# An attention and gated-MLP kernel on one core: a fixed order of all pieces, fewer bound products, and a transpose in two heights

## The chip, the core and the metric

The kernel runs on one core of one Trainium2 chip. A core has five engines that run side by side, each with its own queue of instructions, taken strictly in order: TensorE (PE) multiplies matrices into PSUM, with weight loads (PEld) beside the products; VectorE (DVE) reduces and combines; ScalarE (ACT) applies functions and copies out of PSUM; GpSimd (POOL) works on SBUF; SyncE (SP) here only issues transfers (DMAs). An instruction that waits holds up everything behind it in its queue.

The metric is the device time of one execution in microseconds. Before the change it was 249.93 (median of three runs, 248.54 to 249.93). About one per cent, 2.5 us, is what such a measurement can tell from no change.

## The reference

Two layers follow each other. The first is causal attention for 4 batches of 8 heads, 768 tokens, 64 values per head, in which each query sees only 6 of the 24 chunks of 32 keys: those with the largest upper bound of the score.

```python
ub = sum(max(q * k_min[chunk], q * k_max[chunk]))        # a bound per query and chunk
ub = where(own chunk or earlier, ub, -1e9)
top_chunks = argsort(ub)[-6:]
scores = where(in top_chunks and key <= query, scale * q @ k.T, -1e9)
attn = softmax(scores); x = attn @ v
```

The second layer is a gated MLP over tokens: `h = relu(x @ w_in)`, its halves are u and v; v is normalized over its 512 values, mixed over the tokens by `w_spatial`, a bias is added, and `out = (u * v_mixed) @ w_out`. The result is 4 x 768 x 512 floats.

A query in the first 128 tokens has at most 4 chunks at or before its own, so all of them are among its 6.

## The kernel before

Heads are taken in pairs, so that 2 x 64 values fill 128 rows: 16 pairs, four per batch. The work of a pair is cut into *pieces*, small functions `k_...` with one or a few instructions on one engine. A piece's name is its kind, its pair (or batch) and its part, as in `probs` (4, 512). In the order in which a pair needs them:

- `load`, `cast` (to 16 bits), `turn` and `kT`/`qT`: transposed keys and queries. Pairs 5 to 15 are transposed by a DMA from SP, the others by PE and a copy. `qp` is max(-q, 0).
- `ext` (DVE, L671): maximum and minimum of each chunk of keys. `bounds` (PE, L692 to L702): for each of six tiles of 128 queries, three kinds of products give the upper bounds of 24 chunks; for the first six pairs (`EARLY`) a further one adds a large negative number to chunks past the query (`big` times `far`). `ub` copies the result out of PSUM, and for later pairs adds that number there (`far32`). `top` (DVE) finds the eight largest for tiles 1 to 5, `leave` marks what is not among the first six.
- `pk` (PE) and `mx` (DVE, L792 to L808): the products of queries and keys and their largest value per chunk, kept in `cmax`. The first three pairs do it by another way (`kd`, `fd`, `fr`, `fi`, `fb`).
- `minus` and `kept` (POOL), `shift` (DVE): the softmax's shift is joined to the mask, as one table `bias`.
- `turn_bias` (PE, L826) transposes that table, `bT` (ACT) copies it out. `probs` (PE) are the scores plus mask, `ex` (ACT) their exponentials, `cut` (POOL) the causal mask in the diagonal blocks; it needs the first two parts of `ex`, 0 and 512. `weigh` (PE) multiplies by v, `av`, `sum`, `inv`, `norm` divide by the sums, and `xT` (by a DMA or by `turn_x` on PE and a copy) transposes the result.

When the four pairs of a batch are there, the second layer runs: `hv` and `hu` (the two halves of the first product), `vr` and `uT` (relu), `bn` and `rstd0` to `rstd2`, `vn` (normalizing), `mix` (over the tokens, by the transposed weights `wsT`, which `turn_ws` makes once), `plus` and `gT` (bias and gate), `og` (last product), `oe` (copy out of PSUM) and `od` (store).

Products on PE come in two heights. Those named in `TILED` (L102) use 64 rows, half the array, and stand in pairs on the two halves; all others use 128 rows.

*What sets the order.* `work_list()` (L251) lists 1395 pieces with their engines, an assumed duration, the pieces they follow, and the buffers they fill and read. `Work.order()` (L114) puts them in order. It walks a list: it keeps a clock per engine in assumed times, and whenever an engine is free it takes, of the pieces whose inputs are there and whose buffers can be had, the one with the lowest number in `RANK`. A piece that may run on more than one engine has its engine from a letter of `WHERE`. Each engine's queue is then this order, and each buffer's place is decided on the way (`place`, L139). The chip doesn't keep the assumed times: it keeps the order, and each instruction waits for its true inputs. PSUM holds three buffers `two` and two `mg`; kT and qT have four buffers, loads two.

Of the kernel before, what the change touches and what calls it, by code (L numbers as in the profile page):

```python
# [16 lines left out]
P = 128  # L17
# [66 lines left out]
"""  # L84
WHERE = """
AAAAGAGAGVGVGAAVAGAGAGVVAGAGAGAVVVVVAVAVAAAAAVVAVGGGGVGGAAVAAAAAAAAAAAVVAVAVVAAVAAVVGGGGGVVAAAAA
# [3 lines left out]
class Work:  # L90
# [8 lines left out]
    DELAY = {"PE": 0.25, "DVE": 0.17, "ACT": 0.18, "POOL": 0.14, "SP": 0.0}  # L99
    TILED = ("pk", "probs", "bounds", "turn_bias", "fd", "fb")  # L100
# [12 lines left out]

    def order(self):  # L114

        pieces, n = self.pieces, len(self.pieces)
        users, slot, freed_at, done_at = {}, {}, {}, {}
        slots = {tag: [None] * k for tag, k in self.bufs.items()}
        then, todo, ready_at, begun = [[] for _ in range(n)], [0] * n, [0.0] * n, [False] * n
        for i, (_, _, _, after, new, old, _) in enumerate(pieces):  # L120
            for b in new + old:
                users[b] = users.get(b, 0) + 1
            for a in after:
                then[self.index[a]].append(i)
                todo[i] += 1
        rank, where = [int(x) for x in RANK.split()], iter(WHERE.replace("\n", ""))
        engine = dict(P="PE", V="DVE", A="ACT", G="POOL", S="SP")
        assert len(rank) == n
        for i, (name, on, _, after, new, old, dma) in enumerate(pieces):
            if len(on) > 1:  # L130
                e = engine[next(where)]
                on = {e: on[e]}
# [934 lines left out]
```

## Time and profile before

| what | us |
|---|---|
| median of three runs | 249.93 |
| the profiled execution | 248.22 |
| its span, first to last instruction | 246.5 |
| PE busy | 224.9 |
| VectorE busy | 206.5 |
| ScalarE busy | 191.9 |
| GpSimd busy | 165.9 |

The page gives one execution. Its span is the time between the first and the last instruction, and the execution's own time is 1.7 us longer. Busy time is how long an engine had work in hand, whether or not the end of the kernel waited for that work. The clock that PE was granted is full in all of it. In a row of the timeline stand the start, the length, the engine, the line, the operation, its output and inputs, shapes, a count, and in brackets how long the engine was idle before it and who ended that. Products on PE overlap, so that the distance from one piece's start to the next piece's start, and not the length in the row, is what a piece takes.

### The profile page before, as it was taken

The page shows a single profiled execution, that of the slowest core. Times are in us where ns is not written, and L with a number is a line of the kernel's source. Part 1 is how long each engine was busy: PE and PEld are TensorE (multiplying, and loading weights), DVE is VectorE, ACT ScalarE, POOL GpSimd, SP SyncE. Part 2 cuts the span into 40 slices and gives each one's busy share as a digit, 9 for nine tenths or more (in the row PEclk, how much of TensorE's full clock was granted, in tenths as well). Part 3 has the DMA queues.
Part 4 walks back from the last instruction along what each step waited for, and adds up shares of the span by engine and source line. Part 5 has one row for each costly group of instructions (what it writes and reads, how often), then busy time and mean ns, then how long its engine had stood idle before and what let it go on. Part 6 is the DMA issues. An engine that isn't in the chain of part 4 may idle for free.

```text
span 246.5 us, 9019 instructions
## 1 busy us (share of the span) xinstructions
PE 224.9 (91%) x3780; PEld 144.6 (59%) x3780; DVE 206.5 (84%) x512; ACT 191.9 (78%) x298; POOL 165.9 (67%) x209
## 2 busy tenths in 40 slices
PE   0898778878999999999999999999999999999993
PEld 0656457666755675666665576666745566645551
DVE  4799999999999999799998997899998853349670
ACT  3598887979998999587859897897679969767312
POOL 8879749887785377999965929999926147402160
PEclk9999999999999999999999999999999999999999
DMA  7969996699999949484899997128900010350005
GB/s 189 325 186 201 257 242 127 122 164 241 168 186 235 216 82 187 89 170 112 190 161 271 175 200 125 34 75 140 268 22 19 0 36 0 105 188 0 0 28 227
DMA packets 93895, 35.51 MB, mean 144 GB/s; under 512 B 86208, under 2 KB 90144, under 8 KB 93856
## 3 DMA queue, kind: packets, MB, share of 16 engines
q1 hardware_dynamic: 91568, 31.81, 61.9%
q0 software_dynamic: 2016, 2.75, 6.5%
q8 instruction: 29, 0.48, 0.8%
q10 hardware_dynamic: 272, 0.39, 0.5%
q14 instruction: 10, 0.08, 0.1%
HBM read 24.77 MB, written 6.29 MB: 126 GB/s over the span
## 4 chain that ended last, share of the span: by engine, by line
PE 48%; DVE 28%; ACT 14%; DMA 4%; issue 3%; POOL 2%; DVEq 0%; ACTq 0%
DVE cmax L807 11%; PE mg L1001 11%; ACT pr L871 8%; PE mg L1024 6%; PE mg L885 5%; PE two L856 4%; PE mg L937 3%; PE two L863 3%; DVE stats L954 3%; DVE ext L671 3%; PE two L786 3%; DVE top L715 2%; PE mg L990 2%; DMA k<-in_k_dram 2%; DVE cmax L801 2%
## 5 line engine op out<-in xcount | busy, mean ns | idle before, releaser
L871 ACT ACTIVATE pr<-two 128x1024 f16<-128x1024 f32 (+1 forms) x96 | 85.3, 934 | 5.4 <-PE two L863 4.8
L807 DVE TENSOR_REDUCE cmax<-two 128x24 f32<-128x768 f32 (+4 forms) x104 | 85.3, 843 | 3.5 <-PE two L735 2.0
L856 PE MATMUL two<-qT,kT 64*128 64x128 f16 (+3 forms) x384 | 40.5, 258 | 5.4 <-ACT bT L835 1.9
L863 PE MATMUL two<-bT,member 64*128 64x128 f16 (+1 forms) x512 | 39.7, 233 | 0.0
L877 POOL TENSOR_SCALAR_AFFINE_SELECT pr<-pr 128x768 f16<-128x768 f16 x32 | 27.9, 886 | 9.1 <-ACT pr L871 9.0
L1019 POOL TENSOR_TENSOR vr<-tmp,uT 128x384 f16<-128x384 f32 x27 | 24.5, 922 | 11.9 <-DVE tmp L1012 11.8
L671 DVE TENSOR_REDUCE ext<-kT 128x24 f16<-128x768 f16 x32 | 29.5, 936 | 1.9 <-ACT kT L617 1.7
L1001 PE MATMUL mg<-wsT,vn 128*128 128x384 f16 x168 | 30.2, 327 | 0.0
L856 PEld LDWEIGHTS <-kT 64*128 64x128 f16 x384 | 19.9, 94 | 17.2 <-issue 15.1
L863 PEld LDWEIGHTS <-member 64*128 64x128 f16 x512 | 25.7, 94 | 5.1
L885 PE MATMUL mg<-v,pr 128*128 128x65 f16 x672 | 25.9, 194 | 0.7 <-POOL pr L877 0.5
L786 PE MATMUL two<-kT,qT 64*128 64x384 f16 (+4 forms) x182 | 24.6, 280 | 1.4 <-ACT pr L871 0.5
L885 PEld LDWEIGHTS <-pr 128*128 128x128 f16 x672 | 23.1, 98 | 3.6 <-issue 1.0
L1001 PEld LDWEIGHTS <-vn 128*128 128x128 f16 x192 | 17.7, 98 | 12.2 <-issue 0.6
L990 PE MATMUL mg<-xT,w_in_sb 128*128 128x384 f16 x112 | 22.4, 328 | 0.0
L907 POOL TENSOR_TENSOR x<-av,rc 128x768 f16<-128x768 f32 x11 | 16.2, 1469 | 8.8 <-DVE rc L900 4.9
L732 PE MATMUL two<-kT,qT 64*128 64x128 f16 x192 | 19.6, 221 | 2.3 <-ACT qT L617 1.0
L1024 PE MATMUL mg<-w_out_sb,vr 128*128 128x512 f16 x84 | 20.8, 380 | 0.0
L937 PE MATMUL mg<-w_in_sb,xT 128*128 128x512 f16 x84 | 20.3, 380 | 0.4 <-DVE o L619 0.4
L889 ACT COPY av<-mg 128x390 f32<-128x390 f32 x32 | 15.6, 500 | 6.2 <-PE mg L885 6.0
L954 DVE BATCH_NORM_STATS2 stats<-vr 128x6 f32<-128x512 f32 x24 | 16.6, 692 | 4.0 <-ACT vr L942 2.9
L735 PE MATMUL two<-half_ahead,ident 64*128 64x64 f16 x192 | 19.8, 193 | 0.0
(113 smaller groups left out, 496.8 us busy)
## 6 DMA issues: line engine op xcount, KB each, us to landing
q<-in_q_dram SPq DMA_DIRECT2D x16, 384.0 KB, 6.4
v<-in_v_dram SPq DMA_DIRECT2D x16, 384.0 KB, 5.7
out_dram<-o SPq DMA_DIRECT2D x24, 256.0 KB, 2.1
k<-in_k_dram SPq DMA_DIRECT2D x15, 384.0 KB, 5.7
vr<-in_moe_w_spatial_dram POOLq DMA_DIRECT2D x6, 192.0 KB, 5.6
w_in_sb<-in_moe_w_in_dram POOLq DMA_DIRECT2D x4, 256.0 KB, 8.8
w_out_sb<-in_moe_w_out_dram POOLq DMA_DIRECT2D x4, 128.0 KB, 4.5
k<-in_k_dram ACTq DMA_DIRECT2D x1, 384.0 KB, 4.7
```

Of the source, the lines that this page charges most:

```text
L671: nc.vector.tensor_reduce(held["ext", p][:, m], src, axis=AX.X, op=Alu.min if m else Alu.max, negate=(m == 1))
L786: mm(t[:, h, o:o + before], lhsT=qT[rows[h], c], rhs=kT[rows[h], a * CH:a * CH + before], start=True, stop=True)
L807: nc.vector.tensor_reduce(tops(p)[:, i // 2, :, i % 2, a:z], held["two", (p, u)][:, :, o:o + n].rearrange("p h (c e) -> p h c e", e=CH), a ...
L856: mm(t[:, h, z:z + n * P], lhsT=kT[rows[h], keys], rhs=qT[rows[h], i * P:(i + n) * P], start=True, stop=False)
L863: mm(d, lhsT=member[rows[h], r, keys], rhs=bT[rows[h], m * P:(m + w_) * P].rearrange("c (m s) -> c m s", s=P), start=False, stop=(n == 1 o ...
L871: nc.scalar.activation(out=held["pr", p][:, :, c0:c0 + n], in_=held["two", (p, "e", c0)][:, :, 0:n], func=Act.Exp, scale=scale)
L877: nc.gpsimd.affine_select(out=d, in_=d, compare_op=Alu.is_ge, fill=0.0, base=0, channel_multiplier=-1, pattern=[[0, NT], [1, P]])
L885: mm(a[:, i, :], lhsT=pr[:, at[t, i]:at[t, i] + P], rhs=vp[:, h * NT + t, :], start=(t == 0), stop=(t == i))
L937: mm(t, lhsT=held["xT", b][:, ko, i * P:(i + 1) * P], rhs=w_in_sb[:, ko, DH:2 * DH], start=(ko == 0), stop=(ko == NDO - 1))
L990: mm(t, lhsT=w_in_sb[:, ko, db * P:(db + 1) * P], rhs=held["xT", b][:, ko, s * HS:(s + 1) * HS], start=(ko == 0), stop=(ko == NDO - 1))
L1001: mm(t, lhsT=held["vn", b][:, si, db * P:(db + 1) * P], rhs=wsT[:, si, s * HS:(s + 1) * HS], start=(si == 0), stop=(si == NT - 1))
L1024: mm(t, lhsT=held["vr", ("g", b)][:, ko, i * P:(i + 1) * P], rhs=w_out_sb[:, ko, :], start=(ko == 0), stop=(ko == KO - 1))
```

## The change

Four things change.

1. `Work.order()` no longer walks a list with clocks. `RANK` now holds the place of each piece in one order of all pieces, and the function only reads it off, asserts that inputs come first, and gives each buffer the place whose last use lies furthest back. The numbers in `RANK` and the letters in `WHERE` are new, so nearly every piece moves a few places, and some pieces change engine.
2. `bounds` leaves out the three products of the first tile. Only the `big` times `far` product stays there, now for all pairs.
3. `turn_bias` can use all 128 rows: for those pairs whose `turn_bias` stands between two pieces of the other height in PE's queue, it multiplies by 64 columns of the whole identity and not by the half's own.
4. Assumed durations in `work_list()` are altered; with no clock left in `order()`, they have no effect.

```diff
+    EITHER = ("turn_bias",)
...
     def order(self):
...
-        free = {e: 0.0 for e in self.ENGINES}
-        ready = {e: [] for e in self.ENGINES}
-        events = [(0.0, i) for i in range(n) if todo[i] == 0]
...
+        for (name, on, _, _, _, _, _), at in zip(pieces, rank):
+            result[at] = name, engine[next(where)] if len(on) > 1 else next(iter(on)), at
+        done = set()
+        for at, (name, _, _) in enumerate(result):
+            _, _, _, after, new, old, _ = pieces[self.index[name]]
+            assert all(a in done for a in after) and all(b in slot for b in old), name
+            for b in new:
+                tenants = held[b[0]]
+                free = [(-1 if x is None else last[x], k) for k, x in enumerate(tenants) if x is None or users[x] == 0]
+                assert free, name
+                slot[b] = min(free)[1]
+                tenants[slot[b]] = b
...
     order, slot = work.order()
+    turned = [name for name, e, _ in order if e == "PE"]
+    whole = {name[1] for a, name, z in zip(turned, turned[1:], turned[2:])
+             if name[0] in Work.EITHER and not (a[0] in Work.TILED or z[0] in Work.TILED)}
...
-            each = [(big, far[:, i])] * (p < EARLY) + [(qT[:, c], x[:, 0]), (qp[:, c], x[:, 0]), (qp[:, c], x[:, 1])]
+            each = [(big, far[:, i])] * (p < EARLY or i == 0) + [(qT[:, c], x[:, 0]), (qp[:, c], x[:, 0]), (qp[:, c], x[:, 1])] * (i > 0)
...
-                r = slice(g * D, (g + 1) * D)
-                mm(t[:, g, m * D:(m + 1) * D], lhsT=bias[slot["bias", p]][r, 4 * m:4 * m + 4, :].rearrange("p g c -> p (g c)"), rhs=ident[r, r], start=True, stop=True)
+                r, c = slice(g * D, (g + 1) * D), slice(0, P)
+                if p in whole:
+                    r, c = c, r
+                mm(t[:, g, m * D:(m + 1) * D], lhsT=bias[slot["bias", p]][r, 4 * m:4 * m + 4, :].rearrange("p g c -> p (g c)"),
+                   rhs=ident[r, c] if p in whole else ident[r, r], start=True, stop=True)
```

What moves, in the built order of each engine:

- SP: the first loads were q0, v0, k2, q1, k1, q2 and become q0, q1, k1, k2, v0, q2. The transfer of `member` and the load of the MLP's bias come later.
- POOL: `rows` (which builds `member`) comes after `cast` of q1, k1, k2 and `kd` 0; `cast` of v2 after `kept` 2; `far32` after the cuts of pair 1; the last load of the spatial weights behind `norm` 2.
- ACT: the six parts of `ex` 15 came as 0, 1024, 2048, 1536, 2560, 512 and come as 0, 512, 2048, 1024, 2560, 1536.
- PE: most pieces move by one to six places; `turn_ws` 4 comes ahead of `pk` (6,0) and `weigh` (3,1); `turn_x` 15 comes before the last `og` of batch 2 and not after it.
- Engines: `kT` 0 goes from ACT to DVE and `ub` 3 and 4 from DVE to ACT; `norm` 6 and 7 from POOL to DVE, `norm` 13 from DVE to POOL; `qp` 8 and 13 from ACT to DVE, `qp` 14 back; `oe` (0,1), (0,3), (1,3), (1,4) from DVE to ACT; and 16 pieces of the second layer in batches 2 and 3.

More of the change, by code (lines that the diff above doesn't have):

```diff
@@ L1 @@
-import heapq
 import math
@@ L32 @@
 RANK = """
[51 rows of a table removed]
[51 rows of a table added]
 """
 WHERE = """
-AAAAGAGAGVGVGAAVAGAGAGVVAGAGAGAVVVVVAVAVAAAAAVVAVGGGGVGGAAVAAAAAAAAAAAVVAVAVVAAVAAVVGGGGGVVAAAAA
+VAAAGAGAGAGAGAAVAVAVVGVVAGAGAGVGAVVVAAAAAAAAAAAAVGGGGVGVAAAVAAAAVAAAVVVVAVAVAAAVVVVGGVGVGGAVAVAA
 """
@@ L116, in order @@
         pieces, n = self.pieces, len(self.pieces)
[L117 to L120, printed above, removed]
+        rank, where = [int(x) for x in RANK.split()], iter(WHERE.replace("\n", ""))
+        engine = dict(P="PE", V="DVE", A="ACT", G="POOL", S="SP")
+        assert sorted(rank) == list(range(n))
@@ L121, in order @@
+        users, slot, last, result = {}, {}, {}, [None] * n
+        held = {tag: [None] * k for tag, k in self.bufs.items()}
+        for _, _, _, _, new, old, _ in pieces:
             for b in new + old:
                 users[b] = users.get(b, 0) + 1
[L123 to L132, printed above, removed]
-            pieces[i] = (name, on, rank[i], after, new, old, dma)
-        free = {e: 0.0 for e in self.ENGINES}
-        ready = {e: [] for e in self.ENGINES}
-        events = [(0.0, i) for i in range(n) if todo[i] == 0]
-        t, bus, late, tiled, result = 0.0, 0.0, 0.0, False, []
-        def place(i):
-            got = []
-            if any(b not in slot for b in pieces[i][5]):
-                return None
-            for tag, key in pieces[i][4]:
-                for k, b in enumerate(slots[tag]):
-                    if b is None or freed_at.get(b, t + 1) <= t + 1e-9:
-                        got.append(((tag, key), k))
-                        break
-                else:
-                    return None
-            return got
@@ L153, in begin @@
-        def begin(e):
-            nonlocal bus, late, tiled
-            aside, found = [], False
-            while ready[e] and not found:
-                due, i = heapq.heappop(ready[e])
-                if begun[i]:
-                    continue
-                got = place(i)
-                if got is None:
-                    aside.append((due, i))
-                    continue
-                found = begun[i] = True
-                name, on, _, _, new, old, dma = pieces[i]
-                result.append((name, e, t))
-                took = on[e]
-                if e == "PE" and tiled != (name[0] in self.TILED):
-                    tiled, took = not tiled, took + 0.095
-                free[e] = t + took
-                if dma:
-                    if e == "POOL":
-                        late = max(late, t + took + 0.2)
-                        both = max(0.0, bus - late)
-                        bus += min(both, dma)
-                        late += 4 * dma if dma <= 0.25 * both else 0.75 * both + dma
-                        done = late + 0.8
-                    else:
-                        bus = max(bus, t + took + 0.4)
-                        both = max(0.0, late - bus)
-                        bus += 4 * dma if dma <= 0.25 * both else 0.75 * both + dma
-                        done = bus + 0.8
-                else:
-                    done = t + took + self.DELAY[e]
-                for b, k in got:
-                    slot[b] = k
-                    slots[b[0]][k] = b
-                for b in new + old:
-                    done_at[b] = max(done_at.get(b, 0.0), done)
-                    users[b] -= 1
-                    if users[b] == 0:
-                        freed_at[b] = done_at[b]
-                        heapq.heappush(events, (freed_at[b], -1))
-                for j in then[i]:
-                    todo[j] -= 1
-                    ready_at[j] = max(ready_at[j], done)
-                    if todo[j] == 0:
-                        heapq.heappush(events, (ready_at[j], j))
-            for x in aside:
-                heapq.heappush(ready[e], x)
-            return found
@@ L203, in order @@
-        heapq.heapify(events)
-        while len(result) < n:
-            while events and events[0][0] <= t + 1e-9:
-                i = heapq.heappop(events)[1]
-                if i >= 0:
-                    for e in pieces[i][1]:
-                        heapq.heappush(ready[e], (pieces[i][2], i))
-            while any([free[e] <= t + 1e-9 and begin(e) for e in self.ENGINES]):
-                pass
-            later = [f for f in free.values() if f > t + 1e-9] + [e[0] for e in events[:1]]
-            assert later or len(result) == n, "nothing can go on"
-            t = max(t, min(later, default=t))
+        for (name, on, _, _, _, _, _), at in zip(pieces, rank):
+            result[at] = name, engine[next(where)] if len(on) > 1 else next(iter(on)), at
@@ new lines, in order @@
+        done = set()
[8 more added lines that the diff above has]
+                tenants[slot[b]] = b
+            for b in new + old:
+                users[b] -= 1
+                last[b] = at
+            done.add(name)
@@ L318, in work_list @@
         far_pe = p < EARLY
-        add("bounds", {"PE": (6 * far_pe + 18) * 0.027},
+        add("bounds", {"PE": 0.54 if far_pe else 0.412},
             DUE["bounds"],
@@ L396, in work_list @@
                 add("inv", {"DVE": 0.14}, at, 0, after=[("sum", p, 0)], old=[("rc", (p, 0))])
-                add("norm", {"POOL": 1.6, "DVE": 1.45}, at, 0, after=[("inv", p, 0)], old=[("av", p), ("rc", (p, 0))], new=[("x", p)])
+                add("norm", {"POOL": 1.5, "DVE": 1.15}, at, 0, after=[("inv", p, 0)], old=[("av", p), ("rc", (p, 0))], new=[("x", p)])
                 continue
```

8 lines of the change are left out of this document (4 added, 4 removed), and 102 rows, old and new, of the table RANK.

## The prediction

> **What bounds the kernel now.** I read the page's header, its slices and its chain first, then the busy time by stage, then the waits inside the stages. PE is TensorE, DVE VectorE, ACT ScalarE, POOL GpSimd.
>
> ```profile
> span 246.5 us, 9019 instructions
> ...
> PE   0898778878999999999999999999999999999993
> ...
> DVE  4799999999999999799998997899998853349670
> ...
> PE 48%; DVE 28%; ACT 14%; DMA 4%; issue 3%; POOL 2%; DVEq 0%; ACTq 0%
> ```
>
> PE is below nine tenths in most of the first ten slices (6.2 us each) and full from then on; DVE is full early and thins out after slice 30. The busy time by stage says it in microseconds: the columns are the stage, its length, then busy time of PE, PE's weight loads, DVE, ACT and POOL, the clock, and the DMA.
>
> ```profile
> 5.50:20.00 14.50, 12.14 (x261) 8.81 (x262) 12.35 (x27) 10.68 (x16) 11.91 (x15) 1.00 0.89 241
> 20.00:30.00 10.00, 7.96 (x174) 5.35 (x171) 10.00 (x36) 9.22 (x13) 8.22 (x15) 1.00 1.07 245
> 30.00:40.00 10.00, 8.17 (x206) 6.23 (x206) 9.23 (x22) 8.80 (x13) 6.53 (x8) 1.00 1.10 219
> 40.00:50.00 10.00, 8.73 (x224) 6.72 (x220) 9.96 (x30) 9.09 (x14) 8.33 (x12) 1.00 0.59 116
> 50.00:60.00 10.00, 7.91 (x236) 6.12 (x233) 10.00 (x25) 8.24 (x14) 8.22 (x12) 1.00 1.15 194
> ...
> 70.00:112.00 42.00, 41.58 (x723) 26.11 (x722) 39.65 (x92) 36.45 (x60) 31.07 (x37) 1.00 0.89 160
> 112.00:212.00 100.00, 98.85 (x1589) 61.84 (x1584) 83.86 (x203) 82.74 (x133) 70.44 (x80) 1.00 0.58 113
> 212.00:220.00 8.00, 7.05 (x72) 3.98 (x71) 3.27 (x7) 4.61 (x8) 2.01 (x2) 1.00 0.56 190
> ```
>
> Three stages. From 20 to 60 us DVE is busy 39.2 of 40 us and PE idles 7.2: **DVE sets the pace**. From 70 to 212 PE is busy 140.4 of 142: **PE sets it**, with DVE close beside it up to 112 (2.35 us spare in 42). At 212 to 220 PE loses 0.95 us. A microsecond off PE counts in full after 60 us and not at all before; one off DVE counts before 60.
>
> **The change part by part.** The order of the built kernel, engine by engine, keeps the same 1395 pieces and moves most of them a few places; 29 pieces change engine. PE's products fall from 3780 to 3704.
>
> *First tile's bounds.* For tile 0 only the mask product stays. A pair from the sixth on loses 4 of 36 products, one of the first six loses 6 of 48. The chain has both forms, start, duration, line and count, and a `mix` piece before a tiled and before an untiled piece:
>
> ```profile
> 10.01 0.64 PE two L702 x48
> ...
> 151.79 1.08 PE mg L1001 x6
> ...
> 153.43 0.44 PE two L702 x36
> ...
> 230.74 0.97 PE mg L1001 x6
> ```
>
> 0.44/36 = 12.2 ns a product: 10 pairs x 4 x 12.2 ns = **-0.5 us** where PE is the bound. The early six (6 x 6 x 13.3 ns = 0.48) lie where DVE is, and are worth nothing.
>
> *Turned bias in either height.* PE pays for each change between products on half the rows (two at a time) and on all rows: 1.08 - 0.97 = 0.11 us. The old order has 172 such changes. The new one would have 176, but five `turn_bias` pieces (pairs 7, 8, 10, 12, 15) stand between untiled neighbours and now go untiled, so 166. Six fewer: -0.66. The untiled form costs more itself. The timeline gives its two neighbours:
>
> ```profile
> 155.89 0.25 PE L831 MATMUL two<-ident,bias 64*128 64x64 f16 x6
> 156.08 1.15 PE L1001 MATMUL mg<-wsT,vn 128*128 128x384 f16 x6
> ...
> 163.24 0.83 PE L885 MATMUL mg<-v,pr 128*128 128x65 f16 x21
> 164.00 0.31 PE L786 MATMUL two<-kT,qT 64*128 64x320 f16 x2
> ```
>
> Tiled: 0.19 from start to start, less the 0.11 change, is 0.08 for six. Untiled is not in the trace; the `weigh` row is nearest (all rows, 65 columns): (0.76 - 0.11)/21 = 31 ns, so 0.19 for six, 5 x 0.11 = +0.55 in all. Net **-0.1**, between -0.66 (no dearer than tiled) and +0.8 (dearer twice over).
> The Trainium skill, page "TensorE: Matmul & The Clock Gate", section "The mechanism" of Part 3, says products in different row groups run together; the trace agrees (0.08 for six against 0.19). It prices no change between heights: by it alone the five pieces would be a loss and the sum 0.66 higher. The `mix` rows above decide for the change having a price.
>
> *Pieces that change engine.* Groups by shape, busy time and mean ns behind the bar:
>
> ```profile
> L907 POOL TENSOR_TENSOR x<-av,rc 128x768 f16<-128x768 f32 x11 | 16.2, 1469 | 8.8 <-DVE rc L900 4.9 <-ACT bT L835 3.3 <-ACT pr L871 0.3
> ...
> L907 DVE TENSOR_TENSOR x<-av,rc 128x768 f16<-128x768 f32 x5 | 5.0, 996 | 0.1
> ...
> L619 DVE COPY o<-mg 128x512 f32<-128x512 f32 x6 | 4.1, 678 | 3.4 <-PE mg L1024 3.4
> ...
> L690 DVE TENSOR_SCALAR qp<-qT 128x768 f16<-128x768 f16 x3 | 1.3, 424 | 0.2 <-DMA qT<-q 0.2
> ...
> L619 DVE COPY ub<-two 128x288 f32<-128x288 f32 x2 | 0.9, 446 | 0.0
> ```
>
> `ub` 3 and 4 go from DVE to ACT: -0.9 on DVE before 60, where it is full; ACT has room (8.2 to 9.2 of 10). `norm` 6 and 7 come to DVE (+2.0), `qp` 8 too (+0.4); `oe` (0,1) and (0,3) leave (-1.36). So about +1.0 on DVE around 80 to 125, against the 2.35 of slack to 112 and 16 after. I take **+0.2**; bounds -0.5 (POOL is relieved of 2.9) and +2.8 (third rival). The other swaps lie after 140, where DVE is 16% idle and PE hides them, or in the last 26 us, where the slices show PE full up to the last.
>
> *The start.* SP's loads become q0, q1, k1, k2, v0 (were q0, v0, k2, q1, k1); building `member` on POOL moves behind three casts and `kd`; `kT` 0 moves to DVE, which waited for it:
>
> ```profile
> 7.83 1.81 DVE L671 TENSOR_REDUCE ext<-kT 128x24 f16<-128x768 f16 x2 [1.75 <-ACT kT L617]
> ...
> 8.44 0.82 POOL L621 CAST k<-k 128x768 f16<-128x768 f32 x1 [0.89 <-DMA k<-in_k_dram]
> ```
>
> The wait stays about the same, as it holds the copy and PE's turn (the nearest DVE copy, 678 ns for 512 elements, makes about 1.0 for 768; what that is over ACT's is in the 0.2 below); `clear`, which now stands after the first cast, lies in it. `cast` 2 k goes behind two casts of 0.82, but their data come sooner; `turn` 2 k stays behind `bounds` 0. I charge 0.2, between 0 and two casts, 1.6. Further on SP stops at `load` 4 v until `cast` 2 v, now behind `kept` 2; `load` 6 and the transposes of pair 5 queue behind it. SP already stands there:
>
> ```profile
> 25.23 6.62 SPq L633 DMA_DIRECT2D v<-in_v_dram  x1
> ```
>
> Pair 5 isn't needed by DVE until well past 40, so I charge nothing; `far32` and the bias load also move back, ahead of users that come later still; one more stop of this length is inside the upper bound. Early stage together: -0.9 + 0.2 = **-0.7**, bounds -1.9 (DVE's 0.8 of idle from 20 to 60 and 0.2 of the start also go) and +0.7 (the casts cost 1.6, `ub` gives 0.9).
>
> *First turn of the spatial weights.* `turn_ws` 4 now stands ahead of `pk` (6,0) and `weigh` (3,1), the place of the latter in the old queue and three pieces sooner than the first of its kind; the last of six loads it needs is issued on POOL behind `norm` 2 (1.47) and takes 5.6 us:
>
> ```profile
> vr<-in_moe_w_spatial_dram POOLq DMA_DIRECT2D x6, 192.0 KB, 5.6
> ...
> 63.48 0.51 PE L609 MATMUL mg<-ident,vr 128*128 128x128 f16 x6
> ```
>
> If it is late, PE's queue behind it (`pk` 6, `probs` 4) stops. **+0.1**, between 0 and 1.5 (`norm` 2 in full).
>
> *Before the last batch.* This is the wait in 212 to 220:
>
> ```profile
> 205.42 1.70 POOL L877 TENSOR_SCALAR_AFFINE_SELECT pr<-pr 128x768 f16<-128x768 f16 x2 [0.76 <-ACT pr L871]
> ...
> 211.52 2.49 POOL L877 TENSOR_SCALAR_AFFINE_SELECT pr<-pr 128x768 f16<-128x768 f16 x2 [2.65 <-ACT pr L871]
> ...
> 212.33 0.96 DVE L907 TENSOR_TENSOR x<-av,rc 128x768 f16<-128x768 f32 x1
> ...
> 214.06 0.84 PE L885 MATMUL mg<-v,pr 128*128 128x65 f16 x21 [0.50 <-POOL pr L877]
> ...
> 218.21 0.50 PE L922 MATMUL mg<-ident,x 128*128 128x128 f16 x6
> 219.15 1.67 PE L937 MATMUL mg<-w_in_sb,xT 128*128 128x512 f16 x7 [0.45 <-DVE o L619]
> ```
>
> Old: the slice of `ex` 15 that the cuts need came last, so the cuts came after it, 0.8 us longer than the pair before them while `norm` 14 ran on DVE, and PE waited 0.50 for the second. New: `ex` 15 from 0 and from 512 come first, the cuts run beside the other four, and `weigh` waits for ACT alone. Then `turn_x` 15 moved one `og` (0.87) ahead, so that its copy to SBUF runs beside that `og`: the 0.45 goes. What is late next is PE itself: 28 pieces of `hv`, `hu`, `mix` and `og`, as many as before, to the end. **-0.9**, bounds -0.95 (all that PE idles there) and 0.
>
> Sum: -0.5 - 0.1 + 0.2 - 0.7 + 0.1 - 0.9 = **-1.9** on the span of 246.5, so 244.6. The profiled execution took 248.22, 1.7 more than its span: 246.3. It stood 1.7 under the median shown (249.93, runs 248.54 to 249.93). I predict on the median: 249.93 - 1.9 = **248.0**.
>
> **The rivals.**
> *A, the queues close up.* The early PE idle (9.6 us from 5.5 to 60) is not only DVE's doing; with handovers in a better order PE also draws later work forward, and the 1.6 us idle from 70 to 212 halves. For: many PE pieces move ahead of ones that waited. Against: DVE, full, leaves 0.8 from 20 to 60. Early bound -1.9 in place of -0.7 and -0.8 besides: -3.9, 246.0.
> *B, hidden anyway.* ACT and POOL give back what DVE loses early, so only the late terms stay, and half the wait at 214 with them: -0.5 - 0.1 + 0.2 - 0.4 = -0.8, 249.1. For: ACT is above 8 of 10 through the early stage. Against: DVE at 10.00 of 10. If the untiled `turn_bias` did not save its ten changes, 10 x 0.11 = 1.1 would come back and end here too.
> *C, slower: DVE becomes the bound around 112.* Norms 6 and 7 (1.92) and `qp` 8 (0.42) come onto DVE; if each norm is also held up as the cut at 212 was (0.8), that is 3.9 less the 1.36 of `oe`, about +2.6, and from the point where the 2.35 us of slack is used by the new order PE waits for `shift` and the peaks of pairs 9 to 11 one for one. With the early term at its upper +0.7 and the rest as forecast: -0.5 - 0.1 + 2.6 + 0.7 + 0.1 - 0.9 = +1.9, 251.8; a turn of the weights that comes 1.5 late adds to it.
> The Trainium skill, page "SBUF — State Buffer", section "Who interferes with whom", says that a DVE instruction with two SBUF inputs and a GpSimd one that reads SBUF exclude each other, the later one waiting for the whole of the first. The trace agrees at 212 (2.49 against 1.70, beside a 0.96 norm). C is what this rule would do where DVE is the later one.
>
> **How the numbers follow.** Forecast 248.0: 0.36. A 246.0: 0.26. B 249.1: 0.18. C 251.8: 0.20. One per cent, 2.5 us, is about what a measurement of this kernel tells from no change: under 247.4 and over 252.4. Faster takes most of A and a quarter of the forecast: 0.32. Slower is C's upper half and a little: 0.13. The rest, 0.55, is the same. Range 245.0 to 252.0: it takes in A and C, and leaves out A's lower and C's upper tail.
>
> **What would show it.** PE's products 3704; `turn_bias` of five pairs with 128 rows at about 0.19 us. DVE from 20 to 60 still full, but PE's stage of full slices beginning 0.5 to 1 us sooner. No wait of `weigh` for POOL's cut at the end, and `hv` 3 right behind `og`. Wrong if PE idles over 3 us from 70 to 212 (C, with DVE full there), if `turn_ws` shows a wait for DMA, or if DVE before 60 shows waits for POOL's casts.

## The result and the profile after

The changed kernel takes 251.18 us (median of ten runs, 249.74 to 251.86) against 248.67 for the kernel before in the same session: a ratio of 1.0088, with an interval of 1.0061 to 1.0115. It is 0.9% slower, where 0.8% faster was forecast. (The forecast of 248.0 stood on a median of 249.93 from three runs; ten give 248.67.) The interval is 0.3% to each side, so the difference is clear of no change. The profiled execution took 251.71, its span 249.8.

The page of the changed kernel first: the span, the slices (now 6.2 us each), and the chain that ended last.

```profile
span 249.8 us, 8826 instructions
...
PE   0858888887899999999999999999999999999993
...
DVE  4998989997899999999999999999888836448881
...
PEclk9995999999799999999999999999999999999999
...
PE 52%; DVE 25%; POOL 8%; ACT 6%; DMA 5%; issue 3%; POOLq 0%; ACTq 0%; DVEq 0%
```

Two things are new. The clock, full throughout before, has a slice at five tenths and one at seven. GpSimd holds 8% of the chain, where it held 2%. The same stages as before, with the same columns (the last four of each row are ScalarE's and GpSimd's busy time, the clock and the DMA):

```profile
5.50:20.00 14.50, 9.73 (x180) 7.01 (x180) 14.24 (x26) 8.58 (x13) 10.08 (x13) 0.96 0.89 232
20.00:30.00 10.00, 9.17 (x192) 6.00 (x193) 8.66 (x31) 7.77 (x12) 3.93 (x5) 0.72 0.71 173
...
60.00:70.00 10.00, 8.15 (x182) 6.53 (x180) 8.68 (x29) 7.11 (x12) 4.58 (x7) 0.83 1.00 199
70.00:112.00 42.00, 41.47 (x675) 26.45 (x671) 40.98 (x97) 35.73 (x60) 31.81 (x38) 1.00 1.11 173
112.00:212.00 100.00, 98.99 (x1605) 62.06 (x1602) 88.04 (x203) 85.20 (x139) 74.14 (x83) 1.00 0.62 115
212.00:220.00 8.00, 8.00 (x121) 5.31 (x120) 4.05 (x9) 6.15 (x11) 2.83 (x3) 1.00 0.48 106
```

From 70 us on, the profile is no worse: TensorE idles 1.54 us from 70 to 212 (1.57 before) and nothing from 212 to 220 (0.95 before). The loss is ahead of that. From 5.5 to 20 TensorE is busy 9.73 us in place of 12.14. VectorE is busier there, 14.24 of 14.50, yet did one instruction less (26 against 27): one of them is long. The timeline of the changed kernel at that place, VectorE and GpSimd alone:

```profile
12.76 0.73 POOL L514 MEMSET member<- 1x768 f16 x1
13.44 0.81 POOL L550 CAST q<-q 128x768 f16<-128x768 f32 x1
13.79 3.29 DVE L653 SCALAR_TENSOR_TENSOR bias<-top,ub 128x288 f16<-128x288 f32 x1
14.23 0.90 POOL L669 TENSOR_TENSOR kd<-kT 128x384 f16<-128x384 f16 x1
15.08 0.81 POOL L567 CAST v<-v 128x768 f16<-128x768 f32 x1
15.86 0.90 POOL L669 TENSOR_TENSOR kd<-kT 128x384 f16<-128x384 f16 x1
...
17.00 1.21 DVE L730 TENSOR_REDUCE cmax<-two 128x16 f32<-128x256 f32 x3
```

`leave` 0 takes 3.29 us. It begins inside a cast of GpSimd, and beside it GpSimd runs that cast and three more pieces with no gap, the last until 16.76; `leave` 0 ends 0.32 later. In the kernel before the same instruction, at the same place, takes 0.45, and the piece of GpSimd that begins with it is the longer one (1.21; such a `kd` takes 0.90 or 0.91 elsewhere):

```profile
14.00 0.45 DVE L724 SCALAR_TENSOR_TENSOR bias<-top,ub 128x288 f16<-128x288 f32 x1
14.00 1.21 POOL L740 TENSOR_TENSOR kd<-kT 128x384 f16<-128x384 f16 x1
```

GpSimd has no gap because `rows` (L509 to L514 of the changed kernel, 10.20 to 13.49) now stands between its casts. Behind the long instruction stand VectorE's peaks, and for these TensorE waits (columns: us in total, times, longest):

```profile
PE two L661 <- DVE cmax L730: 1.8, 1, 1.8
```

Right behind that idle time the clock falls to a half, from 18.85 to 25.68. The start of `probs` (0,0), before and after (timelines of TensorE), shows how late the kernel is by then:

```profile
23.63 0.23 PE L856 MATMUL two<-qT,kT 64*128 64x128 f16 x2 [0.81 <-ACT bT L835]
27.33 0.22 PE L788 MATMUL two<-qT,kT 64*128 64x128 f16 x2
```

That is 3.7 us behind, of which 0.5 is `bounds` 1, which now stands ahead of it in TensorE's queue: 3.2 like for like. The kernel also ends 3.2 behind (its last copy out of PSUM starts at 246.04 against 242.82). So all of the net loss is there by 28 us; what comes later adds (to 60 to 70) and gives back about as much.

### The profile page after: what moved, and what is told of

It reads as the page before. It is cut to its first block, busy times and chain, and to the rows that moved or that the text cites. A ratio compares the mean times of both kernels' runs of the same rounds, so it can differ in the third digit from the quotient of the medians.

```text
span 249.8 us, 8826 instructions
## 1 busy us (share of the span) xinstructions
PE 226.4 (91%) x3704; PEld 145.9 (58%) x3704; DVE 212.3 (85%) x515; ACT 189.7 (76%) x297; POOL 165.0 (66%) x207
## 4 chain that ended last, share of the span: by engine, by line
PE 52%; DVE 25%; POOL 8%; ACT 6%; DMA 5%; issue 3%; POOLq 0%; ACTq 0%; DVEq 0%
PE mg L933 11%; DVE cmax L736 8%; PE mg L956 6%; DVE ext L600 5%; PE mg L817 5%; PE mg L869 5%; PE two L788 4%; PE mg L922 4%; PE two L795 4%; PE two L715 3%; DVE bias L653 3%; DMA kT<-k 3%; DVE stats L886 2%; POOL pr L809 2%; DVE cmax L730 2%
## 5 line engine op out<-in xcount | busy, mean ns | idle before, releaser
L809 POOL TENSOR_SCALAR_AFFINE_SELECT pr<-pr 128x768 f16<-128x768 f16 x32 | 29.4, 924 | 11.1 <-ACT pr L803 11.1
L951 POOL TENSOR_TENSOR vr<-tmp,uT 128x384 f16<-128x384 f32 x26 | 25.9, 1006 | 9.7 <-DVE tmp L944 9.3
L817 PE MATMUL mg<-v,pr 128*128 128x65 f16 x672 | 27.3, 195 | 0.8 <-ACT uT L874 0.3
L715 PE MATMUL two<-kT,qT 64*128 64x256 f16 (+4 forms) x182 | 25.4, 283 | 1.7 <-DVE cmax L736 0.9
L817 PEld LDWEIGHTS <-pr 128*128 128x128 f16 x672 | 23.9, 99 | 3.7 <-issue 1.1
L661 PE MATMUL two<-kT,qT 64*128 64x128 f16 x192 | 20.2, 226 | 3.8 <-DVE cmax L730 1.8
L546 ACT COPY o<-mg 128x512 f32<-128x512 f32 x20 | 11.8, 619 | 12.7 <-PE mg L956 12.7
L901 POOL TENSOR_TENSOR rstd<-rstd,mhalf 128x6 f32<-128x6 f32 (+1 forms) x5 | 6.0, 1193 | 22.5 <-DVE rstd L897 21.2
L869 PE MATMUL mg<-w_in_sb,xT 128*128 128x512 f16 x84 | 19.6, 380 | 0.0
L664 PE MATMUL two<-half_ahead,swap 64*128 64x64 f16 x192 | 19.3, 196 | 0.0
```

Of the source, the lines that this page charges most:

```text
L664: mm(t[:, h, d + m * D:d + (m + 1) * D], lhsT=(ident if m == h else swap)[h_rows[h]], rhs=half_ahead[h_rows[h]], start=False, stop=(m == 1))
L715: mm(t[:, h, o:o + before], lhsT=qT[rows[h], c], rhs=kT[rows[h], a * CH:a * CH + before], start=True, stop=True)
L809: nc.gpsimd.affine_select(out=d, in_=d, compare_op=Alu.is_ge, fill=0.0, base=0, channel_multiplier=-1, pattern=[[0, NT], [1, P]])
L817: mm(a[:, i, :], lhsT=pr[:, at[t, i]:at[t, i] + P], rhs=vp[:, h * NT + t, :], start=(t == 0), stop=(t == i))
L869: mm(t, lhsT=held["xT", b][:, ko, i * P:(i + 1) * P], rhs=w_in_sb[:, ko, DH:2 * DH], start=(ko == 0), stop=(ko == NDO - 1))
```

## The experiments

Theory 1: GpSimd's unbroken run keeps `leave` 0 out, and this wait is the loss. Rivals: the half clock is the main price; the order of loads and of GpSimd's queue between 35 and 70 us is; the edits on TensorE cost time. Each kernel was measured beside the kernel before, in 6 to 12 executions. Ratios are to that kernel; 0.1% is 0.25 us, and an interval is 0.2 to 0.4% to each side.

**`rows` early.** The changed kernel, with a few lines that move pieces in the finished order:

```diff
+MOVES = [(('clear',), None), (('rows',), ('far',))]
...
+        for name, behind in MOVES:
+            piece = next(x for x in result if x[0] == name)
+            result.remove(piece)
+            result.insert(1 + [x[0] for x in result].index(behind) if behind else 0, piece)
```

> The changed kernel with two of its 1395 pieces moved: `clear` to the front of the order and `rows` to directly behind `far`, so that GpSimd builds `member` ahead of its casts again, as the kernel before does; everything else stays. Theory 1 (starved `leave`): with `rows` out of the way GpSimd's casts and `kd` pieces no longer stand in one unbroken run beside `leave` 0, which takes 0.45 to 1.2 us in place of 3.29; TensorE no longer idles 1.8 us at 16.45, the half-clock window at 18.9 to 25.7 us goes, and the time falls by 2.5 to 3.5 us against the changed kernel's 251.2, to 247.7 to 248.7. Rival (order of loads between 35 and 70 us): the late loads of pairs 5 to 7 stay, so 1.5 to 2.5 us of the loss stay too, 250 to 250.7, and the half clock at 63 us stays.

Measured: 247.88, ratio 0.9964 (0.9941 to 0.9987). Against the changed kernel that is 1.24% or 3.1 us, from two pieces. Timeline of VectorE and GpSimd:

```profile
13.29 0.91 POOL L676 TENSOR_TENSOR kd<-kT 128x384 f16<-128x384 f16 x1
14.07 0.45 DVE L660 SCALAR_TENSOR_TENSOR bias<-top,ub 128x288 f16<-128x288 f32 x1
14.14 1.06 POOL L574 CAST v<-v 128x768 f16<-128x768 f32 x1
```

`leave` 0 is back at 0.45. It comes 0.07 before GpSimd's next piece, and now that cast is the longer one (1.06 for 0.81). In two later kernels with the same two moves (the last one below, and the one with the edits undone) `leave` 0 began about 0.1 us later, 0.2 inside that cast: it took 0.93 and 0.90 and ended about 0.3 behind the cast, where GpSimd had a gap. So the moves bound the wait and do not always remove it. A half-clock window is left in this profile, at 52 us.

**`leave` late.** Nothing moved on GpSimd; `leave` 0 goes behind the peaks on VectorE:

```diff
+MOVES = [(('leave', 0), ('mx', 0, 2)), (('minus', 0), ('leave', 0))]
```

> The changed kernel with `leave` 0 moved on VectorE to behind `mx` (0,2), with `minus` 0 right behind it; GpSimd's queue keeps `rows` behind the casts and is the same up to `minus` 0. This takes `leave` 0 away from GpSimd's run of four pieces and leaves that run as it is. Theory 1: `leave` 0 falls to 0.45 to 0.7 us, VectorE wins about 2.5 us between 13.8 and 17.1, TensorE's idle time at 16.45 shrinks below 0.8 and the time falls by 1.5 to 3 us, to 248.2 to 249.7 (less than with `rows` early, since `minus` 0 and `shift` 0 come later). Rival (the late casts themselves, or the loads further on, cost the time, and the long `leave` only fills a wait): VectorE or TensorE waits for the casts instead, and the time stays within 0.8 us of 251.2.

Measured: 248.27, ratio 0.9987 (0.9966 to 1.0008), so 2.5 us under the changed kernel. GpSimd's run is the same, 13.54 to 16.86, and nothing on VectorE is long beside it; `leave` 0 takes 0.45 at 17.89. The late casts by themselves cost little here. The clock still falls to a half in this profile, from 20.5 to 23.9 and at 61.5.

**GpSimd stops.** `rows` stays late; GpSimd is made to wait for `leave` 0 two pieces sooner:

```diff
+MOVES = [(('cast', 0, 'v'), ('minus', 0)), (('kd', 1), ('cast', 0, 'v'))]
```

> The changed kernel with `rows` as late as it stands there, and `cast` 0 v and `kd` 1 moved on GpSimd from ahead of `minus` 0 to behind it. `minus` 0 waits for `leave` 0, so GpSimd must stop behind `kd` 2, as it does in the kernel before. Nothing moves on VectorE. Theory 1, that an unbroken run of GpSimd pieces shuts `leave` 0 out: it ends about 0.3 us behind `kd` 2, at 15.2 to 15.5, and takes 1.3 to 1.7 us in place of 3.29; the time falls by 1 to 2.5 us, to 248.7 to 250.2. Rival, that `leave` 0 is long for another reason (its own inputs, or the lateness of `rows` itself): it stays above 2.5 us, and with GpSimd stopped behind it the time is 251 or more.

Measured: 248.48, ratio 0.9995 (0.9968 to 1.0021), 2.3 us under the changed kernel. Timeline:

```profile
13.54 0.81 POOL L557 CAST q<-q 128x768 f16<-128x768 f32 x1
13.83 1.71 DVE L660 SCALAR_TENSOR_TENSOR bias<-top,ub 128x288 f16<-128x288 f32 x1
14.32 0.90 POOL L676 TENSOR_TENSOR kd<-kT 128x384 f16<-128x384 f16 x1
15.63 0.43 POOL L747 TENSOR_SCALAR less<-bias 128x288 f32<-128x288 f16 x1 [0.41 <-DVE bias L660]
```

It begins inside the same cast, and ends 0.32 behind `kd`, the last piece of the shortened run: 1.71 in place of 3.29, nothing else moved on VectorE. This is the sharpest of the three: theory 1 gave 1.3 to 1.7 beforehand.

**The clock.** 40 idle products fill TensorE's gap:

```diff
+        if (p, nm) == (2, "q"):
+            for i in range(40):
+                nc.tensor.transpose(t[:, 6 * P:7 * P], src[:, i % 2], ident)
```

> The changed kernel with 40 more products on TensorE, whose result nobody reads, behind `turn` of q of pair 2: some 2.3 us of work (40 x 57 ns) in the stretch where TensorE idles beside the long `leave` 0. VectorE's and GpSimd's queues stay. It tells the price of the half clock from that of the wait. Theory 1 (the wait of VectorE is the main price, the half clock a lesser one): `leave` 0 still takes about 3.3 us, the pieces at 20 to 30 us are still 2 us or more late, and the time falls by at most 1 us, to 250.2 to 251.2, also where the clock comes back to 1.00 there. Rival (the half clock is the main price): the window at 18.9 to 25.7 goes and 2 us or more with it, to 249.2 or less.

Measured: 249.75, ratio 1.0065 (1.0028 to 1.0102), between what theory 1 said (250.2 to 251.2) and what the rival said (249.2 or less). `leave` 0 is as long as ever and the clock from 20 to 30 is full (timeline, then busy time of the stage):

```profile
13.98 3.35 DVE L656 SCALAR_TENSOR_TENSOR bias<-top,ub 128x288 f16<-128x288 f32 x1
```

```profile
20.00:30.00 10.00, 8.38 (x204) 5.64 (x205) 10.00 (x36) 9.28 (x14) 5.14 (x6) 1.00 0.67 163
```

The start of `probs` (0,0) tells the two prices apart, as TensorE's queue up to it is the same in these kernels but for the idle products. It was 27.33 in the changed kernel; here it is with the 40 products, and with GpSimd stopped (timelines of TensorE):

```profile
26.05 0.22 PE L791 MATMUL two<-qT,kT 64*128 64x128 f16 x2
24.26 0.22 PE L795 MATMUL two<-qT,kT 64*128 64x128 f16 x2
```

A full clock gives back 1.3 us, perhaps a little more, since the idle products may hold up what stands behind them. Shortening the wait as well gives back 1.8 more (2.2 with `rows` early, 23.85).

The executions agree. One fall of the clock to a half for 3.4 us takes 0.007 off an execution's mean granted clock. With GpSimd stopped, five executions at 0.999 to 1.0 took 247.50 to 248.11, four at 0.993 took 248.32 to 248.77, and three at 0.986 took 249.84 to 250.10: about 1 us for each fall. No execution of the changed kernel was above 0.993, and seven of ten were at 0.986 or below; of 87 of the kernel before, measured beside these kernels, one was below 0.997. So the wait is the cause, and the clock about two fifths of its price. Mending the wait gives back 2.3 to 3.1 in all. The ratio of the kernel with 40 products is only 0.23% or 0.6 us under that of the changed one, as two of its nine executions (clock 0.986 and 0.992) took over 252, more than their falls explain.

**`rows` late in the kernel before.** The same one thing the other way round:

```diff
+MOVES = [(('rows',), ('cast', 1, 'k')), (('member',), ('load', 2, 'v'))]
```

> The kernel before with one thing done as in the changed kernel: `rows` on GpSimd behind `cast` 1 k and not ahead of the casts (and the transfer of `member` on SP behind `load` 2 v, so that SP's loads do not wait for it). VectorE's and TensorE's queues stay. `minus` 0 still stands right behind `kd` 2. Theory 1: at about 14 us GpSimd now runs `rows`, `cast` 2 q and `kd` 2 without a gap, `leave` 0 is shut out until `kd` 2 is done, at about 17, and takes over 2.5 us in place of 0.45; the time rises by 1.5 to 3.5, to 250.4 to 252.4. Rival (only casts and `kd` shut it out, or the loss needs the changed kernel's other moves): `leave` 0 under 1.7 us and within 0.8 of 248.9.

Measured: 250.59, ratio 1.0074 (1.0047 to 1.0101). The time is as theory 1 said, and the reason isn't. Timeline, then what TensorE waited for from 12 to 24:

```profile
13.28 0.82 POOL L588 TENSOR_SCALAR_AFFINE_SELECT member<-member 32x768 f16<-32x768 f16 x1
14.09 0.45 DVE L731 SCALAR_TENSOR_TENSOR bias<-top,ub 128x288 f16<-128x288 f32 x1
14.16 1.05 POOL L590 TENSOR_SCALAR_AFFINE_SELECT member<-member 32x768 f16<-32x768 f16 x1
```

```profile
PE mg L659 <- POOL q L628: 2.0, 2, 1.5
```

`leave` 0 came at 14.09, as a piece of GpSimd ended, and went first; TensorE lost 2.0 us to the late `cast` 2 q instead. So theory 1 was too wide: an unbroken run doesn't always keep `leave` out. In the three traces where it was longest (3.29, 3.35, 1.71) it began about 0.3 us inside a piece of GpSimd, and then waited out all that stood behind; where it began less than 0.1 us before GpSimd's next piece (before, `rows` early, here), it took 0.45. Nor does it always wait out the run: in the third kernel of the next group it began at 14.70, 0.63 inside a `kd`, took 0.60, and went ahead of the cast that stood right behind. What decides between the two isn't shown. And a late `rows` has a second price, the casts behind it, in an order that isn't made for it.

**Queues between 35 and 70 us.** On top of `rows` early, `far32` back early; `load` 6 k ahead of `kT` 5; and both, with three loads of `w_in` and `cast` 5 k as early as before:

```diff
+(('far32',), ('cast', 3, 'k'))
...
+(('load', 6, 'k'), ('load', 6, 'q'))
...
+(('far32',), ('cast', 3, 'k')), (('weights', 'in', 0), ('far32',)), (('weights', 'in', 3), ('weights', 'in', 0)),
+(('weights', 'in', 2), ('weights', 'in', 3)), (('cast', 5, 'k'), ('weights', 'in', 1)), (('load', 6, 'k'), ('load', 6, 'q'))
```

> The kernel of the first run (`rows` and `clear` early, median 247.88) with one more piece moved: `far32` (1.8 us on GpSimd, at 41.8 in that run, in a stretch from 37.1 to 54.5 in which GpSimd hardly idles and its casts stand in the chain that ended last) goes back to behind `cast` 3 k, into GpSimd's 3.1 us of idle time at 21.6, as in the kernel before. Theory 2 (GpSimd's full queue between 37 and 54, and with it the late transposes of pairs 5 and 6, is what the new order loses second): `cast` 6 k and the transfers behind it come some 1.8 us sooner, the half clock at 52 us goes, and the time falls by 0.7 to 1.5 us, to 246.4 to 247.2. Rival (the transfers on SP set it, not GpSimd): within 0.4 of 247.9.

> The kernel of the first run with one transfer moved on SP: `load` 6 k from behind `kT` 5 to ahead of it, as in the kernel before, so that it no longer waits (until 40.7) for the buffer that `kT` 5 needs. Theory 3 (SP's order of loads and transposes sets the stretch from 45 to 65): the load is issued at about 34 in place of 42.2 us, and the time falls by 0.7 to 1.5, to 246.4 to 247.2. Rival (GpSimd's full queue sets it; `cast` 6 k stays at about 49.5 in that queue wherever its data are): within 0.4 of 247.9.

> The kernel of the first run with the moves of both other runs of this kind and two more, all to the places they have in the kernel before: `far32` behind `cast` 3 k, three of the four loads of w_in right behind it (each 0.5 to 0.8 us of GpSimd's time, at 31 to 34.8 in that run), `cast` 5 k ahead of `norm` 0 0, `load` 6 k ahead of `kT` 5. Theory 2 and 3 together: GpSimd is some 3 us ahead from 35 on, PE idles less from 45 to 65, no half clock, 246.0 to 246.8, faster than both kernels. Rival (the idle of TensorE there has other causes, such as the exponentials on ScalarE): 247.5 to 248.2.

Measured: 248.05, ratio 0.9974 (0.9950 to 0.9999); 248.10, 0.9977 (0.9951 to 1.0003); 250.16, 1.0042 (1.0014 to 1.0070). The first two do nothing beside `rows` early. The cast that should have come sooner didn't, in either (timelines of GpSimd, `far32` early and then `load` 6 early):

```profile
49.61 0.82 POOL L557 CAST k<-k 128x768 f16<-128x768 f32 x1
```

```profile
49.84 0.82 POOL L557 CAST k<-k 128x768 f16<-128x768 f32 x1
```

It stood at 49.49 with `rows` early alone. Its data had landed by then (at 49.2 and at 43.8), and in both GpSimd runs two pieces of `cut` right up to it: its turn in that queue sets it. The time that `far32` left free GpSimd spent waiting for VectorE, 1.68 us ahead of the `norm` at 46.54. Both moves without the weights weren't tried. The third kernel loses 1.9 us against `rows` early: its weight transfers, issued at 23 to 25, ran beside the loads of pair 4, which landed at 33.4 and 36.7 (29.5 and 32.8 with `rows` early), and TensorE waited for the cast of q:

```profile
PE mg L588 <- POOL q L557: 1.0, 1, 1.0
```

**The edits on TensorE.** Alone in the old order, and undone on top of `rows` early:

```diff
+each = [(big, far[:, i])] * (p < EARLY or i == 0) + [(qT[:, c], x[:, 0]), (qp[:, c], x[:, 0]), (qp[:, c], x[:, 1])] * (i > 0)
...
-    EITHER = ("turn_bias",)
+    EITHER = ()
```

> The kernel before, with its list walk and its order, and the two edits on TensorE alone: the first tile's bounds left out, and the turned bias in either height (there five pairs, 1, 6, 9, 13 and 14, stand between two pieces of full height; 162 changes of height in place of 172). Theory: these two edits work as the prediction's rows say, -0.5 for the products and -0.5 for the heights (ten changes at 0.11 less 5 x 0.11 for the dearer form is about -0.5 at those places), so about -1.0, 247.7 against 248.7, and the new order alone has cost 3.4. Rival (the edits cost, or gain nothing): 248.7 or more, and part of the loss of the changed kernel is theirs.

> The kernel of the first run with the two edits on TensorE undone: the first tile's bounds are computed again (76 products more) and the turned bias always uses half the rows. It tells what part of the gain of the first run (0.36% under the kernel before) is the edits' and what part the order's. Theory (TensorE is the bound from 70 to 212): about 0.6 slower than the first run, 248.3 to 248.7. Rival (in the old order the same edits moved the time by +0.1 with an interval of 0 to 1: others are close behind TensorE): within 0.3 of 247.9.

Measured: 248.99, ratio 1.0020 (1.0000 to 1.0039); 248.22, 1.0001 (0.9976 to 1.0025). In the new order the edits are worth 0.37% or 0.9 us (with both intervals, about 0.1 to 1.8), in the old one nothing: the gain of about 1.0 that was expected there isn't seen. TensorE's waits from 70 to 212 in the old order with the edits:

```profile
PE two L790 <- DVE cmax L811: 0.8, 2, 0.5
PE mg L892 <- ACT uT L949: 0.6, 2, 0.5
```

The work got shorter, and TensorE ran into VectorE and ScalarE sooner: 1.4 us of such waits where the kernel before has 0.8, and from 212 to 220 it idles 1.56 where that one idles 0.95.

**The tail alone.** In the kernel before, the parts of pair 15 in the new order and `turn_x` 15 one `og` sooner:

```diff
+        turn, names = {512: 1536, 1024: 512, 1536: 1024}, [x[0] for x in result]
+        for k, (name, e, at) in enumerate(result):
+            if name[:2] in (("probs", 15), ("ex", 15)):
+                result[k] = name[:2] + (turn.get(name[2], name[2]),), e, at
...
+        i, k = names.index(("og", 2, 2)), names.index(("turn_x", 15))
+        result[i], result[k] = result[k], result[i]
```

> The kernel before with the last step of the prediction alone: for pair 15 the six parts of `probs` and `ex` come as 0, 512, 2048, 1024, 2560, 1536 (they came as 0, 1024, 2048, 1536, 2560, 512), and `turn_x` 15 one `og` sooner. Theory (the 0.95 us that TensorE idles between 212 and 220 count in full): 0.7 to 0.95 faster than the kernel before, 247.9 to 248.2. Rival (others late there take its place): within 0.3 of 248.9.

Measured: 247.58, ratio 0.9960 (0.9940 to 0.9980): 1.0 us. Timeline of GpSimd and TensorE: the cuts are done at 209.9, and the second half of `weigh` follows the first without a wait.

```profile
208.21 1.69 POOL L886 TENSOR_SCALAR_AFFINE_SELECT pr<-pr 128x768 f16<-128x768 f16 x2
...
212.12 1.66 PE L894 MATMUL mg<-v,pr 128*128 128x65 f16 x42
```

**The spatial weights.** With the early stage mended, TensorE stood for the last of these loads (waits of the kernel in which `load` 6 is early):

```profile
PE mg L545 <- DMA vr<-in_moe_w_spatial_dram: 1.4, 1, 1.4
```

On top of `rows` early:

```diff
+(('turn_ws', 4), ('weigh', 3, 1)), (('ex', 4, 2048), ('turn_ws', 4)), (('av', 3, 1), ('ex', 4, 2048)),
+(('wsT', 4), ('av', 3, 1)), (('norm', 2, 0), ('weights', 'ws', 3))
```

> The kernel of the first run with the first turn of the spatial weights put back: `turn_ws` 4 on TensorE from ahead of `pk` (6,0) to behind `weigh` (3,1), its copy `wsT` 4 on ScalarE behind `av` (3,1), and on GpSimd the last load of these weights ahead of `norm` 2. In the kernels whose early stage was mended, TensorE stands there for this transfer: 0.34 us in the first run, 1.38 with `load` 6 early, 1.43 with GpSimd stopped behind `kd` 2. Theory (the prediction's upper bound of 1.5 for this step was real once the early loss no longer hid it): the wait goes and the time falls by 0.3 to 1.2, to 246.7 to 247.6. Rival (something else is late right behind it, the copies on ScalarE or the exponentials): within 0.3 of 247.9.

Measured: 246.30, ratio 0.9912 (0.9885 to 0.9938): 1.3 us under `rows` early (with both intervals, 0.4 to 2.2), and faster than both kernels of this case, by 0.9% and 1.7%. The profile of `rows` early shows only 0.34 us of that wait, and part of the 1.3 is the clock: five of the six executions had 0.998 to 1.0 (with `rows` early five of twelve had 0.997 or more), and among such executions the medians differ by 0.8. TensorE no longer waits for a transfer there; its wait at the turns is for a copy:

```profile
65.84 0.49 PE L545 MATMUL mg<-ident,vr 128*128 128x128 f16 x6 [0.24 <-ACT av L828]
```

## Why the prediction was wrong

The step that failed is *the start*, priced at -0.7. It named the move ("building `member` on POOL moves behind three casts and `kd`") and charged 0.2 for casts that come later. It asked who waits for the casts, and not what VectorE does beside GpSimd when that has no gap. The price was a wait of 2.84 us (3.29 less 0.45) on the engine that the same prediction called the bound up to 60 us, and with TensorE's clock it came to 2.3 to 3.1. The upper bound, +0.7, held no such term. This is a mis-sized term with its sign turned, and the mechanism was at hand: the long cut at 212 was quoted, and rival C was made of it. C put it at norms 6 and 7 around 112 us. There nothing came of it: TensorE idles 0.53 of 42 us from 70 to 112, though VectorE's slack fell from 2.35 to 1.02. That C's 251.8 stands near the measured 251.18 is chance. Of the signs that were named, TensorE's products are 3704 as said, but VectorE is busy only 36.2 of 40 us from 20 to 60 (39.2 before), and TensorE's full slices begin one slice later, not sooner.

Behind the row that C used, the Trainium skill, page "SBUF — State Buffer", section "Who interferes with whom", has the later of the two instructions wait for the whole of the first. The trace differs in size: `leave` 0 waited not for one instruction of GpSimd but for four. Further on in the same trace the wait is for one, as on that page: the `leave` at 128.41 began 0.46 inside a cast, ended 0.32 behind it (0.68 in all), and GpSimd's next piece took 1.08 in place of 0.86.

*The clock* had no term at all. It was full in all of the profile before, and the sum took it as given. Behind the stretch with the wait of 1.8 us it fell to a half, and with that gap filled it didn't.

*First turn of the spatial weights*, +0.1 between 0 and 1.5: the upper bound was nearer. In the changed kernel it can't be seen, since all was late and the turn ran at 66.89, after the last load had landed at 66.33. With the early loss gone it showed as 0.34 to 1.43 us, and mending it gave 1.3, the clock's part included.

*First tile's bounds* and *turned bias*, -0.6 together: 0.9 in the new order. By the prediction's prices it should be about 1.05 there, as undoing the edits brings ten changes of height back (176 for 166) and not six; both lie inside the interval. In the old order they were lost to waits, so that "a microsecond off PE counts in full after 60 us" holds only where VectorE and ScalarE aren't right behind. The untiled `turn_bias` takes 0.17 from start to start, against the estimated 0.19:

```profile
205.04 0.34 PE L762 MATMUL two<-ident,bias 128*128 128x64 f16 x6
205.21 2.11 PE L933 MATMUL mg<-wsT,vn 128*128 128x384 f16 x12
```

*Before the last batch*, -0.9: right. Alone it gave 1.0; in the changed kernel the lag falls by 0.7 between `weigh` (15,0) (+3.9) and the end (+3.2), TensorE idles nothing from 212 to 220, and `weigh` waits for no cut:

```profile
214.41 0.86 POOL L809 TENSOR_SCALAR_AFFINE_SELECT pr<-pr 128x768 f16<-128x768 f16 x1
...
216.61 1.57 PE L817 MATMUL mg<-v,pr 128*128 128x65 f16 x42
```

*Further on SP and POOL*, charged at nothing: half open. `far32` and `load` 6 k, each put back alone, gave nothing; both together, without the weights, weren't tried. The second half clock of the changed kernel (63.22 to 66.64) costs about 1 us by the executions above, and its cause is open: with `rows` early seven of twelve executions had a fall and five had none, so one profile can't tell.

With the two mended, `rows` and the turn of the weights, the new order is 0.88% or 2.2 us faster than the kernel before; the sum said 1.9. Of the terms after 60 us, the edits held in the new order and the step before the last batch held by itself; the +0.2 for pieces that change engine wasn't tried. One early term of the six turned the sign.

## What to carry to other kernels

When pieces are moved on GpSimd, look at what VectorE runs beside them, not only at who waits for the pieces: an instruction of VectorE with two inputs in SBUF that begins inside a piece of GpSimd can wait for the whole run of pieces behind it (it did in three of these traces, and elsewhere for one piece), and a gap in that run can be worth more than its length (0.41 us of it saved 1.58). A loss early in a kernel hides stalls behind it, so after mending it read the waits again before pricing the rest; here a transfer for which the changed kernel shows no wait was worth about 1 us. The mean clock of every execution tells more of a clock's price than one profile. And an order that is tuned as a whole can be worth less than one of its pieces costs: two pieces out of 1395 put back turned +0.9% into -0.4%.

## What was not expected of the hardware

Which of the two goes first turns on tenths of a microsecond. `leave` 0 at 14.00, 14.07 and 14.09, less than 0.1 before GpSimd's next piece, went first and took 0.45; at 13.79, 0.35 inside a piece, it took 3.29. There the run of GpSimd went on without letting VectorE in, each piece at its usual length (0.81, 0.90). At other places VectorE got in behind one piece; why is open.

TensorE's clock fell to a half not after a long pause but after stretches of 3.41 us in which TensorE was part idle. Busy time by stretch in the changed kernel, TensorE alone, the two stretches ahead of each fall (at 18.85 and 63.22):

```profile
12.02:15.44 3.42, 2.52 (x38) 1.00 1.08 282
15.44:18.85 3.41, 1.52 (x41) 1.00 0.60 146
56.40:59.81 3.41, 2.63 (x59) 1.00 1.02 124
59.81:63.22 3.41, 2.07 (x48) 1.00 1.20 235
```

1.52 and 2.07 of 3.41 us busy came ahead of a fall, and so did 2.37 and 2.15 in two of the mended kernels; each fall lasted 3.4 or 6.8 us. In steps of 3.41 us, counted back from its fall behind the last instruction (at 246.94), the kernel before has a stretch of 2.14 (52.38 to 55.79) with no fall. So the busy share of one such stretch doesn't decide it alone; what does wasn't tried.
